# The last three stores of an attention-and-MLP kernel, issued by ScalarE instead of SyncE

## The chip, the cores and the metric

The kernel runs on one core of a Trainium2 chip. The metric is device time in microseconds of one execution. A run of the kernel is also profiled once; the profile's span goes from the first to the last instruction of the program, and the time of the execution is a little longer than that.

The engines are named as the profile names them: PE is TensorE (PEld its weight loads), DVE is VectorE, ACT is ScalarE, POOL is GpSimd, SP is SyncE. A letter q behind an engine's name marks its sequencer: the part that waits, branches, and issues DMAs. SyncE has no arithmetic; everything it does is its sequencer's.

## The reference

Two layers in a row, batch 4, 8 heads, 768 positions, 48 values a head (model width 384):

```python
# linear attention with a per-channel decay w and a bonus u for the present position
for t in range(S):
    kt, vt, rt = k[:, :, t], v[:, :, t], r[:, :, t]
    cur = np.einsum('bhd,bhe->bhde', u[None] * kt, vt)
    y[:, :, t] = np.einsum('bhd,bhde->bhe', rt, state + cur)
    state = w[None, :, :, None] * state + np.einsum('bhd,bhe->bhde', kt, vt)
...
# x is y with the heads side by side: [4, 768, 384]
xt = x.transpose(0, 2, 1)
h = xt @ U @ V                      # mixes positions, rank 32
u = x + h.transpose(0, 2, 1)
ch = np.maximum(u @ w_ch1, 0.0) @ w_ch2   # 384 -> 1536 -> 384
return u + ch
```

All inputs and the output are float32. The decays w are drawn between 0.85 and 0.95.

## The kernel before

The attention is done in chunks of 128 positions, six to a batch (`NCH`), with matmuls inside a chunk and a small state from chunk to chunk. The MLP is done in halves of a batch: a step of 384 positions (`TB`), two steps to a batch (`NTB`), three blocks of 128 rows to a step (`TPB`). For each of 12 slices of the hidden width, `m_1` multiplies (in two float parts, "high" and "low"), ScalarE takes the ReLU (line 1080), VectorE takes the remainder of it (line 1081), and `m_2` adds the second product to three accumulators in PSUM. TensorE works on the MLP of one batch while the attention of the next is slipped in between.

The order of the instructions is made by a planner written in the kernel (class `Plan`). Every piece of work is an `op` with an engine, an estimated duration and the buffers that it reads and writes; `schedule` plays them through and picks an order, and `run` then emits the instructions in that order, each engine's program being one fixed sequence. The helper `dma` (line 364) makes an op of a transfer: `eng` says whose queue issues it, SyncE's unless it says "ACT". ScalarE's queue is used so far only by a few loads at the very start. The synchronisation itself, semaphore waits of the issuing engine, is added by the framework. There are eight semaphores for the completion of DMAs, given out in turn to whatever queue issues; before a semaphore is used again, the issuing engine checks that its last transfer has landed.

The end of a step is in `m_2`. For the last step of the last batch, the matmuls are ordered block by block, so that the three accumulators end one after the other. VectorE adds each to its rows x (line 1120), and a store of 128 rows of 1536 bytes takes the result from x to the output (line 1124). The op of the store reads x, so SyncE waits for VectorE's addition before it issues.

Behind the plan there is a second way of computing everything, for decays that the fast path can't handle. `flags` (line 465, placed in the schedule at the start of the second batch) compares w with 0.7 and 1.0 and writes 1 into `flag` when any value lies outside; with the inputs here it is 0. After the plan, line 1312 has every engine load the flag from SBUF into a register (its own `TENSOR_LOAD`), and line 1313 opens `tc.If(rv == 1)` around `slow_path()`. Each engine branches for itself: with a flag of 0 it jumps over its part of `slow_path` to a short block, which the profile also puts on line 1313. There the semaphores are raised to the values that they would have after the other path. SyncE has eight such instructions, one for each DMA semaphore, each of which first checks that the transfers issued so far have landed; ScalarE, VectorE and TensorE have one each, for their own semaphore. Line 1340 is the end of the program: SyncE checks all semaphores once more, two to an instruction (the last pair has ScalarE's), and then all engines meet twice at a barrier.

`slow_path` (line 1151) itself begins with loads of w and u on SyncE's queue (lines 1163 and 1164), goes through all positions in a loop with VectorE alone, writes the attention's result to DRAM, and then runs the same MLP functions for each batch, with its stores to the output on SyncE's queue as well. None of it is executed here.

Of the kernel before, what the change touches and what calls it, by code (L numbers as in the profile page):

```python
# [46 lines left out]
class Plan:  # L47
# [28 lines left out]
    def op(self, eng, ns, fn, w=(), r=(), alt=(), lock=False, dma=0.0, rows=0, late=0.0, tiled=False, dk=0.0):  # L76


        if self.direct:
            fn()  # L80
            return None
        o = Op()
        o.n = len(self.ops)
        o.key = (self.key + dk, o.n)
        o.ways = [(eng, ns, fn, lock)] + list(alt)
        o.dma, o.rows, o.late, o.tiled = dma, rows, late, tiled
        o.deps, o.behind, o.allocs, o.bufs = set(), set(), [], []
        for acc, write in [(a, False) for a in r] + [(a, True) for a in w]:
            b, sub = acc if isinstance(acc, tuple) else (acc, None)
            if not b.uses and b.tag:  # L90
                o.allocs.append(b)
                ring = self.rings.setdefault(b.tag, {"order": [], "next": 0, "free": [(0.0, "")] * b.bufs, "last": None})
                ring["order"].append(b)
            elif b.tag and b.uses[0][0] is not o:
                o.behind.add(b.uses[0][0])
            for p, s, pw in b.uses:
                if (write or pw) and (s is None or sub is None or s == sub) and p is not o:
                    o.deps.add(p)
            b.uses.append((o, sub, write))
            if b not in o.bufs:  # L100
                o.bufs.append(b)
                b.left += 1
        self.ops.append(o)
        return o
# [184 lines left out]
def rwkv_moe(ctx: ExitStack, tc: tile.TileContext, r, k, v, w, u, U, V, w1, w2, out):  # L289
    nc = tc.nc  # L290
    B, H, S, D = r.shape
# [13 lines left out]
    NTB = S // TB  # L305
    TPB = TB // 128
# [25 lines left out]
    def bank(tag, name):  # L332
        return Buf(ps, [128, 512], F32, tag, {"mm": 2, "acc": 3}.get(tag, 1), name)
# [7 lines left out]
    def whole(*args, **kw):  # L341

        opened.clear()
        return nc.tensor.matmul(*args, **kw)  # L344
# [19 lines left out]
    def dma(fn, w_, r_, rows, run, eng="SP", ns=470, dk=0.0, late=0.0, either=False):  # L364

        q = nc.scalar if eng == "ACT" else nc.sync
        return op(eng, ns, lambda: fn(q), w_, r_, dma=rows * max(1.08 if run < 500 else 0.96, run / 400),
                  rows=rows, late=late, dk=dk, alt=[("ACT", ns, lambda: fn(nc.scalar), False)] if either else ())
# [617 lines left out]
    def inside(b, t):  # L986

        return b < B and (t == 0 or b == 0)
# [96 lines left out]
    def m_2(b, t, f, first, last):  # L1085

        hh, hl = hs.pop((b, t, f))
        for i in range(TPB):
            n = b * NCH + t * TPB + i
            if first:  # L1090
                ops[n] = bank("acc", f"p2_{n}_{f}")

        def high(i, pt):
            ts_ = slice(i * 128, (i + 1) * 128)
            for half in range(2):
                whole(pt.t[:, :DM], lhsT=hh.t[:, ts_], rhs=W2[f].t[:, half], start=(first and not gates and half == 0), stop=False)

        def low(i, pt):
            ts_ = slice(i * 128, (i + 1) * 128)
            whole(pt.t[:, :DM], lhsT=hl.t[:, ts_], rhs=W2[f].t[:, 0], start=False, stop=last > 0)  # L1100
        def gate(i, pt):
            whole(pt.t[:, :DM], lhsT=V3.t[:, (t * TPB + i) * 128:(t * TPB + i + 1) * 128], rhs=Gs[b].t, start=True, stop=False)
        gates = f == 0 and inside(b, t)
        if gates:
            for i in range(TPB):
                pt = ops[b * NCH + t * TPB + i]
                pe(MM, lambda i=i, pt=pt: gate(i, pt), [pt], [Gs[b], V3])
        parts = [(part, m, h, i) for part, m, h in ((high, 2, hh), (low, 1, hl)) for i in range(TPB)]
        if b == B - 1 and t == NTB - 1 and last:

            parts.sort(key=lambda p: p[3])
        for part, m, h, i in parts:
            n = b * NCH + t * TPB + i
            pe(m * MM, lambda part=part, i=i, pt=ops[n]: part(i, pt), [ops[n]], [h, W2[f]])
        if last:
            for i in range(TPB):
                n = b * NCH + t * TPB + i
                x, pt = xs[n], ops[n]
                s0 = (t * TPB + i) * 128
                on_dve(384, lambda e, x=x, pt=pt: e.tensor_tensor(x.t, pt.t[:, :DM], x.t, ALU.add), [x], [pt])  # L1120
                left[n] = left.get(n, NFT) - last
                if not left[n]:
                    del left[n]
                    dma(lambda q, x=x, s0=s0: q.dma_start((out[b] if b < B else slow_out[0])[s0:s0 + 128, :], x.t), [], [x],
                        128, 1536, ns=375)

    left = {}

    def mlp_units(b):

# [12 lines left out]
    slow_out = [None]  # L1143
# [7 lines left out]
    def slow_path():  # L1151
        st = xbuf([128, EQ, D], F32, "bl", 5, "s_state").t
        tmp = xbuf([128, EQ, D], F32, "bl", 5, "s_tmp").t
        wb = work.tile([128, D], F32, tag="xl", name="s_w", bufs=NXS)
        uu = work.tile([128, D], F32, tag="dv", name="s_u", bufs=2)
        rb = xpool.tile([128, TS, D], F32, tag="uTh", name="s_r", bufs=2)
        kb = xpool.tile([128, TS, D], F32, tag="uTh", name="s_k", bufs=2)
        pb = xpool.tile([128, TS, D], F32, tag="uTl", name="s_p", bufs=2)
        vb = work.tile([128, TS, EQ], F32, tag="ldv", name="s_v", bufs=3)
        yb = work.tile([128, TS, EQ], F32, tag="ldr", name="s_y", bufs=NR)  # L1160
        dg = work.tile([128, TS], F32, tag="dg", name="s_dg", bufs=2)
        for i in range(128 // H):
            nc.sync.dma_start(wb[i * H:(i + 1) * H], w)
            nc.sync.dma_start(uu[i * H:(i + 1) * H], u)
        nc.vector.memset(st, 0.0)
        rf, kf, vf = (a.rearrange("b h s d -> (b h) s d") for a in (r, k, v))

        def de(ap):
            return ap.unsqueeze(1).broadcast_to([128, EQ, D])

        def ee(ap):
            return ap.unsqueeze(2).broadcast_to([128, EQ, D])

        with tc.For_i(0, S, TS) as t0:
            for q in range(NQ):
                ps_ = slice(q * BH, (q + 1) * BH)
                nc.sync.dma_start(rb[ps_], rf[:, ds(t0, TS), :])
                nc.sync.dma_start(kb[ps_], kf[:, ds(t0, TS), :])
                nc.sync.dma_start(vb[ps_], vf[:, ds(t0, TS), q * EQ:(q + 1) * EQ])
            nc.vector.tensor_mul(pb, kb, uu.unsqueeze(1).broadcast_to([128, TS, D]))  # L1180
            nc.vector.tensor_mul(pb, pb, rb)
            nc.vector.tensor_reduce(dg, pb, AX.X, ALU.add)
            for i in range(TS):
                nc.vector.tensor_mul(tmp, st, de(rb[:, i, :]))
                nc.vector.tensor_reduce(yb[:, i, :], tmp, AX.X, ALU.add)
                nc.vector.scalar_tensor_tensor(yb[:, i, :], vb[:, i, :], dg[:, i:i + 1], yb[:, i, :],
                                               ALU.mult, ALU.add)
                nc.vector.tensor_mul(st, st, de(wb))
                nc.vector.tensor_mul(tmp, de(kb[:, i, :]), ee(vb[:, i, :]))
                nc.vector.tensor_add(st, st, tmp)  # L1190
            for q in range(NQ):
                for b in range(B):
                    p0 = q * BH + b * H
                    dst = xd[b, ds(t0, TS), :].rearrange("t (h q e) -> h t q e", h=H, q=NQ)[:, :, q, :]
                    nc.sync.dma_start(dst, yb[p0:p0 + H])
        with tc.For_i(0, B, 1) as b:
            for i in range(NCH):
                n = B * NCH + i
                x = xbuf([128, DM], F32, "x", NX, f"x_{n}")
                nc.sync.dma_start(x.t, xd[ds(b, 1), i * C:(i + 1) * C, :].rearrange("o t c -> (o t) c"))  # L1200
                xs[n] = x
            c_g(B)
            for i in range(NCH):
                c_u(B, i)
                c_ut(B, i)
            slow_out[0] = out[ds(b, 1)].rearrange("o s c -> (o s) c")
            for f in mlp_units(B):
                f()
# [61 lines left out]
    for b in range(B):  # L1270
        n0 = b * NCH
        last = b + 1 == B
        t = begin[b]
# [39 lines left out]
    with tc.If(rv == 1):  # L1313
        slow_path()
# [30 lines left out]
```

## Time and profile before

| what | us |
|---|---|
| median of three runs | 438.2 (436.89 to 439.71) |
| the profiled execution, its time | 439.95 |
| the profiled execution, its span | 437.9 |
| TensorE busy (matmuls) | 419.4 |
| VectorE busy | 267.8 |
| ScalarE busy | 142.9 |
| GpSimd busy | 55.6 |

The profile has a page, which sums up one execution, and a trace behind it, which answers questions: a timeline of a stretch, all instructions of a line, the chain of work that ended last, DMA packets by queue. A row of a line's answer reads: line, engine, operation, tiles, count, shortest/median/longest duration in ns, start of the first and of the last in us, and the shapes. A row of DMA packets reads: queue, kind, number of packets, megabytes, and their share of the 16 DMA engines' time in the stretch that was asked for; packets of the kind "instruction" carry the engines' own program code.

Two things are to be known of it here. Instructions of a sequencer (semaphore checks, branches, flag loads, issues of DMAs) are not counted as busy, and the chain of work that ended last is followed back from the last instruction that does count. And a sequencer instruction's start is when it is taken up, so a wait shows as a long instruction or as a hole in front of it.

The granted TensorE clock, in the page's row by 40 slices, is at nine tenths or more from the sixth slice (about 55 us) to the last but one, and 0.984 on average over the span.

### The profile page before, as it was taken

Reading aid. Unit: us, or ns where it says so; the run is one execution under the profiler, and the core shown is the slowest. Engines: PE = TensorE matmul, PEld = TensorE weight load, DVE = VectorE, ACT = ScalarE, POOL = GpSimd, SP = SyncE. Lnnn points to the kernel's source line nnn. Section 1 sums busy time; section 2 is a strip of 40 time slices with the busy share of each in tenths; the row PEclk is TensorE's granted clock in tenths of the full one; section 3 lists DMA queues with packets and bytes.
Section 4 is the critical chain, followed back from the end, with each engine's and each line's share of the span. In section 5 each row is a group of like instructions: output and inputs, shape, how many; then the busy total and the mean of one; then the engine's idle time right before and its main releaser. Section 6 shows DMA issues by size and latency. Waiting matters only on the chain.

```text
span 437.9 us, 12193 instructions
## 1 busy us (share of the span) xinstructions
PE 419.4 (96%) x5125; PEld 399.8 (91%) x5125; DVE 267.8 (61%) x602; ACT 142.9 (33%) x399; POOL 55.6 (13%) x92
## 2 busy tenths in 40 slices
PE   8889999999999999999999999999999999999991
PEld 8678899889999999999999999999999999999991
DVE  6979699999887757767775456567522351122121
ACT  1679679934421213121112221222112131111110
POOL 2651151223110002011100001101100000000000
PEclk9989699999999999999999999999999999999998
DMA  9979999654466876744586653231100510001001
GB/s 145 162 162 340 335 199 222 103 84 83 81 88 139 148 146 117 136 87 76 105 168 102 96 147 56 48 64 30 55 2 1 98 65 1 0 0 55 1 0 61
DMA packets 178975, 43.93 MB, mean 100 GB/s; under 512 B 168993, under 2 KB 175650, under 8 KB 178914
## 3 DMA queue, kind: packets, MB, share of 16 engines
q1 hardware_dynamic: 174162, 42.20, 46.9%
q10 hardware_dynamic: 4752, 0.89, 1.5%
q8 instruction: 42, 0.69, 0.7%
q14 instruction: 19, 0.16, 0.1%
HBM read 36.57 MB, written 6.49 MB: 98 GB/s over the span
## 4 chain that ended last, share of the span: by engine, by line
PE 81%; DVE 8%; ACT 3%; DMA 3%; POOL 1%; issue 1%; SPq 0%; ACTq 0%; DVEq 0%; POOLq 0%
PE p L344 64%; PE pav L787 5%; PE pav L793 4%; PE pu L344 3%; DVE raw_w L528 2%; DVE raw_w L525 2%; PE pab L751 2%; DMA ld<-in_r_dram 1%; DMA ld<-in_v_dram 1%; PE pab L766 1%; PE wake L344 1%; DVE hl L1081 1%; PE pG L958 1%; ACT dv L681 1%; POOL dv L671 1%
## 5 line engine op out<-in xcount | busy, mean ns | idle before, releaser
L344 PE MATMUL p<-uTh,w1s 128*128 128x384 f32 x576 | 148.2, 338 | 0.0
L1081 DVE SCALAR_TENSOR_TENSOR hl<-p,hh 128x384 fp32r<-128x384 f32 x96 | 53.2, 554 | 119.3 <-ACT hh L1080 119.0
L344 PE MATMUL p<-w2s,hh 128*128 128x384 f32 x576 | 120.3, 340 | 0.6 <-ACT hh L1080 0.6
L1080 ACT ACTIVATE hh<-p 128x384 fp32r<-128x384 f32 x96 | 47.2, 491 | 210.3 <-PE p L344 208.7
L344 PEld LDWEIGHTS p<-uTh,w1s 128*128 128x128 f32 x576 | 102.9, 188 | 0.8
L344 PEld LDWEIGHTS p<-w2s,hh 128*128 128x128 f32 x576 | 99.8, 188 | 2.8 <-ACT hh L1080 0.9
L344 PE MATMUL p<-uTl,w1s 128*128 128x384 f32 x288 | 96.4, 335 | 0.0
L344 PE MATMUL p<-w2s,hl 128*128 128x384 f32 x288 | 65.8, 335 | 0.0
L344 PEld LDWEIGHTS p<-uTl,w1s 128*128 128x128 f32 x288 | 54.0, 188 | 0.0
L344 PEld LDWEIGHTS p<-w2s,hl 128*128 128x128 f32 x288 | 51.4, 188 | 0.0
L787 PE MATMUL pav<-vsw,am 64*64 64x48 f32 x384 | 33.0, 226 | 0.6 <-DVE am L885 0.5
L793 PE MATMUL pav<-S,rT 48*64 48x48 f32 x704 | 32.0, 222 | 0.9 <-issue 0.9
L787 PEld LDWEIGHTS pav<-vsw,am 64*64 64x64 f32 x384 | 26.7, 137 | 6.1 <-issue 4.1
L751 PE MATMUL pab<-rT,kT 48*64 48x64 f32 x768 | 31.2, 228 | 0.3 <-DVE rT L721 0.2
L793 PEld LDWEIGHTS pav<-S,rT 48*64 48x64 f32 x704 | 27.9, 139 | 1.0 <-issue 1.0
L751 PEld LDWEIGHTS pab<-rT,kT 48*64 48x64 f32 x768 | 25.1, 137 | 1.5 <-DVE rT L721 0.5
L787 PE MATMUL pav<-ldv,am 64*64 64x48 f32 x320 | 26.5, 222 | 0.0
L787 PEld LDWEIGHTS pav<-ldv,am 64*64 64x64 f32 x320 | 21.5, 134 | 4.7 <-issue 3.9
L885 DVE TENSOR_TENSOR am<-pab,mask 128x256 f32<-128x256 f32 x48 | 19.7, 417 | 6.8 <-PE pav L793 6.2
L661 POOL MEMSET ks<- 128x128 f32 x24 | 4.9, 205 | 133.2 <-PE pab L766 66.8
L766 PE MATMUL pab<-ldv,ks 64*48 64x48 f32 (+1 forms) x576 | 21.0, 212 | 0.0
L926 ACT ACTIVATE SW<-S,wm 112x48 f32<-112x48 f32 x48 | 12.2, 324 | 21.3 <-DVE S L913 20.0
(127 smaller groups left out, 515.5 us busy)
## 6 DMA issues: line engine op xcount, KB each, us to landing
raw_w<-in_moe_w_ch_dram SPq DMA_DIRECT2D x24, 384.0 KB, 7.4
out_dram<-x SPq DMA_DIRECT2D x24, 192.0 KB, 2.0
ldr<-in_r_dram SPq DMA_DIRECT2D x20, 192.0 KB, 3.3
ldk<-in_k_dram SPq DMA_DIRECT2D x20, 192.0 KB, 3.6
ldv<-in_v_dram SPq DMA_DIRECT2D x20, 192.0 KB, 3.6
bl<-in_r_dram SPq DMA_DIRECT2D x79, 48.0 KB, 2.6
bl<-in_k_dram SPq DMA_DIRECT2D x79, 48.0 KB, 2.5
vsw<-in_v_dram SPq DMA_DIRECT2D x42, 48.0 KB, 3.2
```

Of the source, the lines that this page charges most:

```text
L344: return nc.tensor.matmul(*args, **kw)
L525: nc.vector.scalar_tensor_tensor(word(0), word(1), -2 ** 31, word(0), ALU.bitwise_and, ALU.bitwise_or)
L528: nc.vector.scalar_tensor_tensor(word(0), word(1), 3, word(0), ALU.logical_shift_left, ALU.bitwise_or)
L661: op("POOL", 250, lambda: nc.gpsimd.memset(ks.t[:, :, D:], 0.0), [(ks, "pad")], [])
L751: return [lambda q=q, i=i: nc.tensor.matmul(pt.t[(i ^ j) * C2:(i ^ j) * C2 + C2, q * C2:(q + 1) * C2], lhsT=kT.t[rows, q, i * C2:(i + 1) * ...
L766: return nc.tensor.matmul(pt.t[j * HP:j * HP + m, SU + q * D:SU + (q + 1) * D], lhsT=ks.t[half, 2 * q + j, :m], rhs=vt()[half, 2 * q + j, ...
L787: return nc.tensor.matmul(to(q, j, i), lhsT=am[j].t[half, q, :], rhs=vsw[n].t[half, q, :] if j else vt()[half, 2 * q, :], start=(row == RO ...
L793: return nc.tensor.matmul(to(q, row, i), lhsT=rT.t[rows, q, i * C2:(i + 1) * C2], rhs=St[n, i].t[rows, q, :], start=False, stop=(row == RO ...
L885: on_dve(256, lambda e: e.tensor_tensor(am.t, abs_[n][j].t[:, :SU].rearrange("p (h t) -> p h t", h=NP), mask_.unsqueeze(1).broadcast_to([1 ...
L926: nc.scalar.activation(dec.t[:, q], new.t[:, q], AF.Copy, scale=wm.t[:, q])
L1080: on_act(384, lambda: nc.scalar.activation(hh.t, pt.t[:, :TB], AF.Relu), [hh], [pt])
L1081: on_dve(384, lambda e: e.scalar_tensor_tensor(hl.t, pt.t[:, :TB], 0.0, f32(hh.t), ALU.max, ALU.subtract), [hl], [pt, hh])
```

## The change

The op of the store names a queue: ScalarE's for the last step of the last batch (`b == B - 1 and t == NTB - 1`, three stores), SyncE's for the 21 others. The instruction that a store emits is also kept in a list, `stored`. In `slow_path`, the first load gets a manual dependency on the last three entries of that list: until now the stores of both paths went through one queue.

```diff
-                    dma(lambda q, x=x, s0=s0: q.dma_start((out[b] if b < B else slow_out[0])[s0:s0 + 128, :], x.t), [], [x],
-                        128, 1536, ns=375)
+
+                    dma(lambda q, x=x, s0=s0: stored.append(q.dma_start((out[b] if b < B else slow_out[0])[s0:s0 + 128, :], x.t)), [], [x],
+                        128, 1536, ns=375, eng="ACT" if b == B - 1 and t == NTB - 1 else "SP")
 
     left = {}
+    stored = []
...
         for i in range(128 // H):
-            nc.sync.dma_start(wb[i * H:(i + 1) * H], w)
+            d = nc.sync.dma_start(wb[i * H:(i + 1) * H], w)
+
+            for o in stored[-TPB:] if i == 0 else ():
+                tc.add_manual_dep(d.ins, o.ins.name,
+                                  mybir.DependencyInfo(mybir.DependencyClass.Sync, mybir.DependencyReason.DATA),
+                                  reason="stored before the other path's results")
             nc.sync.dma_start(uu[i * H:(i + 1) * H], u)
```

## The prediction

> **What bounds the kernel now.** I read the page first (busy shares, then the chain that ended last), then the same chain in order of time from 341 us on, then the end engine by engine.
>
> ```profile
> span 437.9 us, 12193 instructions
> PE 81%; DVE 8%; ACT 3%; DMA 3%; POOL 1%; issue 1%; SPq 0%; ACTq 0%; DVEq 0%; POOLq 0%
> 341.42 87.62 PE p L344 x505
> 429.06 0.56 DVE x L1120
> ```
>
> TensorE carries the chain. Its last piece runs 87.62 us without a wait, and the chain ends with VectorE's third addition at 429.06 + 0.56 = 429.62 us. But the span is 437.9 us. So 8.3 us lie behind the last arithmetic, in work the page doesn't count as busy: issues of DMAs, reads of the flag, jumps, semaphore checks. The change touches this tail alone, so the tail needs its own reading. First the stores, from the timeline of the last microseconds (start, duration) and from the answers on line 1124:
>
> ```profile
> 425.93 0.49 ACT L1080 ACTIVATE hh<-p 128x384 fp32r<-128x384 f32 x1 [2.63 <-PE p L344]
> 428.01 1.60 DVE L1120 TENSOR_TENSOR x<-p,x 128x384 f32<-128x384 f32 x3 [1.00 <-PE p L344]
> 428.60 2.09 SPq L1124 DMA_DIRECT2D out_dram<-x  x3
> 430.33 0.36 SPq L1124 DMA_DIRECT2D out_dram<-x  x1
> DMA to landing us min/median/max: 2.1/2.1/2.1
> L1124 SPq DMA_DIRECT2D out_dram<-x x3: 333/344/368, 393.4 to 394.3; - x3
> ```
>
> SyncE issues the three last stores from 428.60 to 430.69 us. The fifth row belongs to the third store alone: it starts at 430.33 and has landed 2.1 us later, at 432.4. So the output is complete 5.5 us before the span ends. SyncE's job before these was the first half's stores, over at 394.3 + 0.37 = 394.7; between 394.7 and 428.6 it has nothing to do.
>
> ScalarE has nothing behind 425.93 + 0.49 = 426.4 us. Now the flag (the answer on the tile flag), which every engine reads on line 1312 before it jumps over the path not taken:
>
> ```profile
> L473 DVE CAST flag<-outside x1: 141/141/141, 106.4 to 106.4; 1x1 int32<-1x1 f32 x1
> L1312 POOLq TENSOR_LOAD <-flag x1: 498/498/498, 352.9 to 352.9; - x1
> L1312 ACTq TENSOR_LOAD <-flag x1: 476/476/476, 425.9 to 425.9; - x1
> L1312 PEldq TENSOR_LOAD <-flag x1: 487/487/487, 427.1 to 427.1; - x1
> L1312 DVEq TENSOR_LOAD <-flag x1: 795/795/795, 429.1 to 429.1; - x1
> L1312 SPq TENSOR_LOAD <-flag x1: 577/577/577, 430.7 to 430.7; - x1
> ```
>
> The flag is ready at 106.5 us, and each engine reads it as soon as its own program arrives there: GpSimd at 352.9, long before the end. SyncE arrives last, at 430.7, because its stores stand in front. Then the jump on line 1313 (the branch, and the first checks behind it), with SyncE's eight checks split by two windows, its seventh check alone, and the end on line 1340:
>
> ```profile
> L1313 ACTq COMPARE_BRANCH  x1: 50/50/50, 426.5 to 426.5; - x1
> L1313 ACTq EVENT_SEMAPHORE  x1: 17/17/17, 427.0 to 427.0; - x1
> L1313 PEldq COMPARE_BRANCH  x1: 3507/3507/3507, 427.7 to 427.7; - x1
> L1313 PEldq EVENT_SEMAPHORE  x1: 51/51/51, 431.2 to 431.2; - x1
> L1313 SPq COMPARE_BRANCH  x1: 50/50/50, 431.4 to 431.4; - x1
> L1313 SPq EVENT_SEMAPHORE  x4: 17/17/17, 434.3 to 434.5; - x4
> L1313 SPq EVENT_SEMAPHORE  x4: 17/17/17, 436.3 to 436.6; - x4
> L1313 SPq EVENT_SEMAPHORE  x1: 17/17/17, 436.5 to 436.5; - x1
> L1340 SPq EVENT_SEMAPHORE  x10: 17/28/28, 436.6 to 437.9; - x10
> ```
>
> SyncE jumps at 431.4, does its first check only at 434.3 (a hole of 2.9 us), makes four checks, and has a second hole from 434.5 to 436.3 (1.8 us). The checks are for the DMA completion semaphores; the instruction records name them, and the fifth to seventh are those of the three last stores. All three had landed by 432.4, so neither hole is a wait for a transfer. In each hole the DMA answer shows an instruction packet, in a stretch that has nothing else (432.5 to 432.7, then 434.5 to 435.0):
>
> ```profile
> q14 instruction: 1, 0.01, 9.6%
> q14 instruction: 1, 0.01, 4.9%
> ```
>
> So I read both holes as SyncE waiting for code behind its jump. What ends last is SyncE's private tail: read 430.7, jump 431.4, code, checks, end 437.9, 7.2 us in all. TensorE's own jump is over at 431.2, ScalarE's takes from 426.5 to 427.0.
>
> A page of the Trainium skill says the same of jumps (Runtime: NRT & Kernel Launch, Instruction fetch mechanics): code is fetched sequentially, and a taken branch whose target lies outside the window already fetched stalls for a DMA fetch. This trace agrees for SyncE (2.9 us) and TensorE (3.5 us), and shows a near target for ScalarE (0.5 us).
>
> **The change, part by part.**
>
> *SyncE loses three issues, and the checks of their semaphores that stand before two of them.* Its program then goes from 394.7 straight to line 1312. Flag read 0.58, branch 0.05, first hole 2.9, four checks 0.2, second hole 1.8: 5.5 us, over by about 400.2, under TensorE's 87.62 us piece. The cover is 28 us wide. Then SyncE stands at the fifth check and waits for the first of the moved stores to land. Of its 7.2 us, what stays on the path is what comes after the third store's check: 437.9 − 436.5 = 1.4 us.
>
> *ScalarE gains three issues, behind 426.4 us,* when its last activation is done. No activation queues behind them; only its flag read, jump and end do. Each issue waits for the same addition as before. Before, the three took:
>
> ```profile
> L1124 SPq DMA_DIRECT2D out_dram<-x x24: 333/371/1090, 136.0 to 430.3; - x24
> L1124 SPq DMA_DIRECT2D out_dram<-x x1: 1090/1090/1090, 429.1 to 429.1; - x1
> q8 instruction: 1, 0.02, 11.8%
> q14 instruction: 1, 0.01, 5.2%
> L651 SPq DMA_DIRECT2D bl<-in_k_dram x3: 467/468/1545, 121.0 to 122.0; - x3
> q8 instruction: 1, 0.02, 29.2%
> L618 ACTq DMA_DIRECT2D ld<-in_k_dram x3: 374/437/621, 0.8 to 5.7; - x3
> L630 ACTq DMA_DIRECT2D vsw<-in_v_dram x6: 602/638/705, 1.3 to 9.8; - x6
> ```
>
> The median store issues in 0.37 us, but the second of the last three took 1.09. The two packet rows (428.6 to 429.2) show why I don't expect that to go: two packets of code start there. The two rows below are a like case: of three loads the one at 122.0 took 1.55 against 0.47, with a code packet in 121.7 to 122.0. TensorE's jump at 427.7, which calls for its code, is not changed. So on ScalarE I take the same issue times as on SyncE: 428.60 to 430.69, third landing at 432.4. The bounds: the stall vanishes, then the third store starts at its addition's end, 429.62, and lands 2.1 later at 431.7 (0.7 earlier); or an issue on ScalarE costs what its dearest one did, 0.71 against 0.36, then 3 × 0.35 = 1.05 us later, at 433.5. I take no difference, as the nearest rows of the same engine (374 to 621 for line 618) hold SyncE's 371 at their low end and the forms that were dearer have smaller pieces.
>
> *ScalarE's tail moves behind the stores:* 430.7 + 0.58 (the dearer read) + 0.1 + 0.5 = 431.9 us, still before the landing at 432.4. TensorE is through at 431.2, VectorE stops at 429.62 plus its own read and jump:
>
> ```profile
> L1313 DVEq EVENT_SEMAPHORE  x1: 21/21/21, 430.9 to 430.9; - x1
> ```
>
> So the third landing is late next, with ScalarE half a microsecond behind it, and TensorE 1.2.
>
> *The manual dependencies* on the first load of the other path stand inside the branch not taken: no cost, unless they act outside it (a rival). *The list* of stores is Python, at build time. The planner's order up to the last additions stays, since the stores come after everything and have one queue each.
>
> **The sum.** End = 432.4 (landing) + 1.4 to 1.5 (what stands behind the check) = 433.9 against 437.9: 4.0 us less. The profiled execution took 439.95 us, 2.05 over its span; that part stays, so 436.0. The median of the three runs is 438.2 (436.89 to 439.71), the profiled one lies 1.75 above it; from the median I get 438.2 − 4.0 = **434.2 us**, 0.9% less.
>
> A rule of the Trainium skill speaks against so much (DMA: Bandwidth & Descriptors, Issuing engines are not separate DMA queues): all issuing engines feed the same 16 DMA engines, and another one saves only the sequencer's time for the issue. What that would give here is rival 4. I hold to 4.0, because what SyncE is freed for is the jump, and the two holes behind it (2.9 and 1.8 us) are longer than the issues (2.09).
>
> **The rivals.**
>
> 1. *The issue stall goes too.* Third landing 431.7 or so, end 0.7 earlier: 433.5 us. For it: the stall belongs to a moment, and ScalarE's queue might meet the code packets otherwise. Against: the same moment, the same transfers. Chance 0.17.
>
> 2. *ScalarE's jump now stalls.* Its program grows by three issues and the checks before them, so its target may fall outside the fetched code. With SyncE's hole: 431.4 + 2.9 = 434.3 us. Of SyncE's tail, the 0.9 us of line 1340 that follow its check of ScalarE would come after that (an estimate, as two thirds of the 1.3 us from 436.6 to 437.9): 435.2, a gain of 2.7, so 435.5 us. Against it: the 0.5 us jump before, over only a few dozen instructions of ScalarE. The skill's rule on branches (same page as above) is what would do this. Chance 0.09.
>
> 3. *Waiting SyncE doesn't fetch ahead,* so the second hole (1.8 us) opens after the landing. 434.2 + 1.8 = 436.0 us. Against: a code packet moves at 427.5 to 427.7, when ScalarE has jumped and stands at the end, so a waiting engine's next code seems to come. The row names no engine, though:
>
> ```profile
> q14 instruction: 1, 0.01, 15.4%
> ```
>
> Chance 0.07.
>
> 4. *Only the issues are saved:* SyncE still doesn't read before the additions, and comes at 428.6 rather than 430.7. The end moves by the 2.09 us of issues: 436.1 us. Against: the flag is ready at 106.5, and GpSimd read it at 352.9, as soon as its work was done. The rule on issuing engines (same skill, DMA page, above) would give this. Chance 0.03.
>
> 5. *The other side: the new dependency holds SyncE before its flag read,* on line 1312, rather than inside the branch. Then it can't read before the third landing: 432.4 + 7.2 = 439.6, 1.7 us later than now, 439.9 us. It decides from a wait that ends after 430.7, SyncE's present arrival. Against: the dependency is hung on an instruction behind the branch. Chance 0.04.
>
> That the stores don't move at all, I can exclude: the condition names the last batch and the last half, three blocks of 128 rows.
>
> **How the numbers follow.** My forecast's chance is 0.58, the rivals' 0.17, 0.09, 0.07, 0.03 and 0.04; 0.02 is for what I don't see. The time is the likeliest case's, 434.2. Its own range is 433.5 to 435.3, from a landing between 431.7 and 433.5. The whole range takes in rivals 1 to 4, and 0.8 us below rival 1, since the median of three runs that span 2.8 us can well lie that far off: 432.7 to 436.2. One per cent, about what a measurement of this kernel can tell from no change, is 4.4 us, so 433.8 is the bound. The forecast lies 0.4 us short of it, a third of it falls beyond by the spread of the runs (0.58 × 0.33 = 0.19), of rival 1 some 0.8 (0.14), and 0.04 of the rest: 0.37 faster. Slower by over 1% (442.6) needs more than rival 5: 0.03. Within 1%: 0.60.
>
> **What would show it.** In the profile of the changed kernel SyncE's flag read and branch should stand near 395 us, its checks 1 to 4 before 401, and checks 5 to 8 close behind the landing, near 432.5, with no hole between. The three stores should be ScalarE's, from 428.6 to about 430.7, one of them near 1.1 us. ScalarE's read should come at about 430.7, its jump take 0.5. The stretch behind VectorE's last addition should shrink from 8.3 to about 4.3 us, and everything before 428 stay as it is. I'm wrong if SyncE's read still comes behind 428 us, if ScalarE's branch takes microseconds, or if a second hole follows the landing.

## The result, and the profile after

| | median of 12 runs, us | lowest to highest | profiled execution: time, span |
|---|---|---|---|
| before | 438.94 | 436.89 to 440.63 | 439.95, 437.9 |
| changed | 435.48 | 433.17 to 436.61 | 435.4, 433.5 |

The ratio is 0.9931, with a 95% interval from 0.9911 to 0.995: 3.0 us less, between 2.2 and 3.9. The medians differ by 3.5 us. The forecast was 434.2 us (0.9% less), in a range from 432.7 to 436.2.

The changed kernel's page begins with

```profile
span 433.5 us, 12193 instructions
```

and its chain of work, in order of time, has as its last long piece (start, duration):

```profile
339.19 87.62 PE p L344 x505
```

The end of the arithmetic and the stores, from the timeline of its last microseconds (start, duration; the last row is the third store alone):

```profile
425.79 1.60 DVE L1120 TENSOR_TENSOR x<-p,x 128x384 f32<-128x384 f32 x3 [1.00 <-PE p L344]
426.38 2.21 ACTq L1125 DMA_DIRECT2D out_dram<-x  x3
428.20 0.39 ACTq L1125 DMA_DIRECT2D out_dram<-x  x1
```

And from the answers on line 1125, all three stores by duration (shortest, median, longest in ns), and the landing of the third:

```profile
L1125 ACTq DMA_DIRECT2D out_dram<-x x3: 373/389/1206, 426.4 to 428.2; - x3
...
DMA to landing us min/median/max: 3.4/3.4/3.4
```

The last addition ends at 425.79 + 1.60 = 427.39 us. I call the rest of the span the tail: 433.48 − 427.39 = 6.1 us, where it was 437.94 − 429.62 = 8.3 before (spans to a hundredth from the trace). So the tail is 2.2 us shorter, not 4.4, which is what the two spans differ by. The other 2.2 us are no part of the change: TensorE's long last piece lasts 87.62 us in both, but starts at 339.19 instead of 341.42. Two more profiles of the kernel before, below, have their additions up to 2.6 us earlier than its first one, so the way there varies. The granted TensorE clock of the first 60 us varies with it. It was 0.91 in the first profile of the kernel before and 1.00 in this one, and 1.00 in both from 60 to 425 us. Over the six profiles of the two kernels, the last addition ends between 426.9 and 427.4 us where the first 60 us were granted 0.97 or more, and between 428.6 and 429.6 us where they were granted 0.91 or 0.94. No run here sets the clock, so that it is the cause is not shown.

Next, SyncE and ScalarE. Their flag reads (the answer on the tile flag):

```profile
L1319 SPq TENSOR_LOAD <-flag x1: 558/558/558, 392.5 to 392.5; - x1
...
L1319 ACTq TENSOR_LOAD <-flag x1: 545/545/545, 428.6 to 428.6; - x1
```

Their jumps and checks, and the end of TensorE's jump (the answers on line 1320, SyncE's checks in two windows):

```profile
L1320 SPq COMPARE_BRANCH  x1: 50/50/50, 393.2 to 393.2; - x1
L1320 SPq EVENT_SEMAPHORE  x4: 17/17/17, 396.0 to 396.4; - x4
L1320 SPq EVENT_SEMAPHORE  x4: 17/17/17, 429.1 to 431.7; - x4
L1320 ACTq COMPARE_BRANCH  x1: 62/62/62, 429.2 to 429.2; - x1
L1320 ACTq EVENT_SEMAPHORE  x1: 17/17/17, 429.7 to 429.7; - x1
L1320 PEldq EVENT_SEMAPHORE  x1: 51/51/51, 429.1 to 429.1; - x1
```

And SyncE's end (line 1347, from its first and from its second check on):

```profile
L1347 SPq EVENT_SEMAPHORE  x10: 17/28/28, 431.8 to 433.4; - x10
L1347 SPq EVENT_SEMAPHORE  x9: 17/28/28, 432.2 to 433.4; - x9
```

SyncE reads and jumps at 392.5 and 393.2, right behind its last remaining store, and its 2.9 us hole (393.2 to 396.0) lies under TensorE's work. It then stands at its fifth check until 429.1, when the first moved store has landed, and passes the third store's check at 431.7. ScalarE does the three issues, reads at 428.6 and is through its jump at 429.7. The end hangs on the landing, as forecast. But the landing took 3.4 us, not 2.1, and from the check at 431.66 to the span's end it takes 1.8 us, not 1.4: there is a step of 0.4 us between the first and second check of line 1347 (431.8 and 432.2), where the others take 0.06 to 0.09.

The semaphore of the third store tells what was late. A transfer raises it by one for each of its sixteen parts (the trace has sixteen rises for each of the three stores). Fifteen came between 430.03 and 430.18, that is 1.8 to 2.0 us behind the issue. The sixteenth came at 431.65. The DMA packets that start from 429.8 to 430.6, when nearly all of the stores is out, show what shares the DMA engines with it:

```profile
q8 instruction: 1, 0.02, 8.2%
q10 hardware_dynamic: 5, 0.01, 6.0%
q14 instruction: 2, 0.02, 6.0%
```

Five packets of the stores start in that stretch (queue q10, ScalarE's), next to one packet of 16 KB and two of 8 KB of program code. The big one starts 0.7 us after TensorE has come out of its jump. The packet records tell more of the late part. Its eight rows of 1536 bytes start at 430.143 us, just as the first 8 KB packet (429.839 to 430.146) ends, and are done at 431.09. Three of them take 0.19 to 0.27 us instead of 0.07 while the two other code packets are under way (430.34 to 430.79 and 429.86 to 430.91). So the late part waits behind code packets of both sizes.

### The profile page after: what moved, and what is told of

It is laid out like the page before. It is cut to its first block, busy times and chain, and to the rows that moved or that the text cites. A ratio compares the mean times of both kernels' runs of the same rounds, so it can differ in the third digit from the quotient of the medians.

```text
span 433.5 us, 12193 instructions
## 1 busy us (share of the span) xinstructions
PE 414.6 (96%) x5125; PEld 394.8 (91%) x5125; DVE 267.7 (62%) x602; ACT 143.3 (33%) x399; POOL 56.6 (13%) x92
## 4 chain that ended last, share of the span: by engine, by line
PE 80%; DVE 12%; DMA 3%; SPq 2%; ACT 1%; POOL 1%; issue 1%; POOLq 0%
PE p L344 64%; PE pav L787 4%; PE pav L793 3%; DVE raw_w L528 3%; PE pu L344 3%; DVE raw_w L525 2%; SPq L618 2%; PE pab L751 2%; DMA ub<-in_u_dram 1%; PE pab L766 1%; DVE hl L1081 1%; DMA ldk<-in_k_dram 1%; PE pG L958 1%; DVE w2s L549 1%; DMA wT<-in_w_dram 1%; DVE uTl L1013 1%
## 5 line engine op out<-in xcount | busy, mean ns | idle before, releaser
L793 PE MATMUL pav<-S,rT 48*64 48x48 f32 x704 | 31.1, 218 | 0.9 <-issue 0.9
L793 PEld LDWEIGHTS pav<-S,rT 48*64 48x64 f32 x704 | 27.0, 135 | 1.1 <-issue 1.1
```

The costliest lines, as they stand in the source:

```text
L793: return nc.tensor.matmul(to(q, row, i), lhsT=rT.t[rows, q, i * C2:(i + 1) * C2], rhs=St[n, i].t[rows, q, :], start=False, stop=(row == RO ...
```

## The experiments

My theory: the gain is SyncE's read and jump, taken out of the tail; what is missing of the forecast is program code being fetched, which holds up one sixteenth of the stores and costs a step at a page edge. The rivals were that ScalarE's queue is the better (or the worse) one for the stores by itself, and that the steps between SyncE's checks are waits.

Each row gives, from the trace, the tail (last addition's end to the span's end), the landing of the third store counted from the last addition's end, and what lies behind the landing; times are ratios to the kernel before.

| kernel | tail, us | third landing, us | behind it, us | ratio (95% interval) |
|---|---|---|---|---|
| before, three profiles | 8.32, 8.08, 8.82 | 2.85, 2.67, 4.07 | 5.5, 5.4, 4.8 | |
| changed, three profiles | 6.09, 5.00, 5.80 | 4.26, 3.17, 3.96 | 1.84, 1.84, 1.84 | 0.9931 (0.9911 to 0.995) |
| third_on_sync | 7.83 | 1.99 | 5.8 | 1.0017 (0.9996 to 1.0037) |
| near_code | 5.23 | 3.65 | 1.58 | 0.9934 (0.9909 to 0.9959) |
| no_branch | 3.05 | 2.15 | 0.90 | 0.9889 (0.9858 to 0.992) |
| edge_moved | 6.31 | 2.88 | 3.4 | 0.9972 (0.9951 to 0.9994) |
| after_edge | 5.41 | 3.95 | 1.46 | 0.9914 (0.9882 to 0.9946) |
| code_later_8 | 4.00 | 2.54 | 1.46 | 0.9941 (0.9909 to 0.9973) |
| code_later_18 | 5.77 | 4.32 | 1.46 | 0.9925 (0.9905 to 0.9946) |

**One store left on SyncE (third_on_sync).**

```diff
-  eng="ACT" if b == B - 1 and t == NTB - 1 else "SP"
+  eng="ACT" if b == B - 1 and t == NTB - 1 and i < TPB - 1 else "SP"
```

> The changed kernel with the third of the three last stores back on SyncE's queue; the first two stay on ScalarE's. My theory: the gain comes from SyncE being free to read the flag and jump 28 us early, and one store left on it takes nearly all of that back. SyncE then issues at the third addition's end (or up to 0.7 us later, if the issue is stalled there too), and the whole tail of 7.2 us follows: stretch from the last addition's end to the span's end 7.6 to 8.3 us, a flag read of SyncE behind the additions, time 438.2 to 438.9 against 438.9 of the kernel before. Rival: ScalarE's queue is the better one for each store by itself. Then two thirds of the gain of 3.5 us stay, 436.6 us.

Its third store in the timeline:

```profile
428.42 0.33 SPq L1125 DMA_DIRECT2D out_dram<-x  x1
```

SyncE's flag read, then its jump and checks (the last row: the first seven of the eight):

```profile
L1319 SPq TENSOR_LOAD <-flag x1: 543/543/543, 428.8 to 428.8; - x1
L1320 SPq COMPARE_BRANCH  x1: 50/50/50, 429.4 to 429.4; - x1
L1320 SPq EVENT_SEMAPHORE  x8: 17/17/17, 432.6 to 434.8; - x8
L1320 SPq EVENT_SEMAPHORE  x7: 17/17/17, 432.6 to 433.1; - x7
```

With a single store left, SyncE's read, its jump (hole of 3.1 us) and its checks with a second hole (433.1 to 434.8) are back behind the additions. The tail is 7.8 us, and the time is that of the kernel before, a gain of more than 0.04% being outside the interval. Two of the three stores went through ScalarE as in the changed kernel, and brought nothing. So it isn't the queue that pays. The third store, issued by SyncE at once, landed in 2.0 us, without the second store's stall in front of it.

**The page edge in the kernel before (edge_moved).**

```diff
             nc.sync.dma_start(uu[i * H:(i + 1) * H], u)
+        for i in range(10):
+            nc.sync.dma_start(uu[i * H:(i + 1) * H], u)
```

> The kernel before, with ten more loads of u on SyncE's queue inside the path not taken (loads of the same values to the same place, never executed). They move SyncE's eight checks behind the branch by ten instructions. My theory: the second hole in SyncE's tail (1.8 us behind the fourth check) is a page edge of its code that falls four instructions behind the jump's target; moved by ten, the edge lies in front of the target, the first hole (2.9 us) stays, the eight checks follow each other in 0.1 us steps, and the tail is 6.5 us instead of 8.3: time 437.1 us against 438.9. Rival: the second hole is a wait for something that ends at that time (a transfer or another engine); then it stays where it is, tail 8.3 us, time 438.9.

SyncE's branch and its eight checks:

```profile
L1315 SPq COMPARE_BRANCH  x1: 50/50/50, 431.2 to 431.2; - x1
L1315 SPq EVENT_SEMAPHORE  x8: 17/17/17, 433.9 to 434.4; - x8
```

The first hole stays (431.2 to 433.9), the second is gone: eight checks in 0.5 us. The tail is 2.0 us shorter than in the first profile of the kernel before, and the time 0.3% less (0.06 to 0.5%). Instructions that are never executed made the kernel faster, by where they put the others. The second hole is a page edge of SyncE's code.

**The same in the changed kernel (after_edge).** The edit is the same, in the changed kernel.

> The changed kernel with the ten never executed loads of u in the path not taken, as in the run with the moved edge. In three profiles of the changed kernel 1.83 us lie between the third landing and the end, where I had put 1.45; the whole difference is one step of 0.4 us instead of 0.07 between two checks of SyncE, nine instructions behind its jump's target. My theory: that is a page edge again, with the next page already there, and it costs 0.33 us by itself. Moved by ten, it lies in front of the target; all checks behind the landing follow at 0.06 to 0.08 us, and 1.45 us lie between landing and end. Tail 4.6 to 5.7 us as the landing falls (3.2 to 4.3 us behind the last addition), time about 0.4 us under the changed kernel's, 0.992 of the kernel before. Rival: the step is a wait at that check (it names VectorE's flag read or a DMA); then it stays.

SyncE's last four checks behind the jump, and its end:

```profile
L1322 SPq EVENT_SEMAPHORE  x4: 17/17/17, 428.2 to 430.6; - x4
L1349 SPq EVENT_SEMAPHORE  x10: 17/28/28, 430.7 to 432.0; - x10
```

All steps are 0.06 to 0.07 us now, and 1.46 us lie behind the landing, where three profiles of the changed kernel have 1.84. So an edge costs 0.33 us even where the next page had more than 30 us to arrive. third_on_sync agrees on the place. Its SyncE has two instructions ahead of the branch that it doesn't have in the changed kernel (a check and an issue), and its hole lies behind the seventh check, where the step of the changed kernel lies behind the ninth. The ratio, 0.9914, is the lowest of all kernels that keep the second path; its interval overlaps the changed kernel's, so the times alone don't tell the two apart.

**The landing from run to run (after_2, after_3, before_2, before_3).** Unchanged kernels.

> The changed kernel once more, for its tail alone. My theory: the third store's landing is what the tail hangs on, and fifteen of its sixteen parts land 1.9 us behind the issue; the sixteenth depends on whether TensorE's second packet of code meets it, so the tail should be either near 4.4 to 5 us or near 6, and differ from run to run. Rival: the landing is always 3.4 us; then the tail is 6.0 to 6.2 us again.

> As the run before it: tail near 4.4 to 5 us or near 6 by my theory, 6.0 to 6.2 us by the rival.

> The kernel before once more. My theory: its tail hangs on SyncE's own read, jump and two holes, not on any landing, so it is 8.2 to 8.4 us again, whatever the third store does. Rival: it varies by a microsecond or more as the code packets fall.

> As the run before it: a tail of 8.2 to 8.4 us by my theory, a microsecond or more off by the rival.

The third store alone, in the second profile of the changed kernel:

```profile
L1125 ACTq DMA_DIRECT2D out_dram<-x x1: 390/390/390, 429.3 to 429.3; - x1
...
DMA to landing us min/median/max: 2.5/2.5/2.5
```

The landing is 2.5 us behind the issue here, 3.2 in the third profile, 3.4 in the first, and the changed kernel's tail follows it: 5.00, 5.80, 6.09. What lies behind the landing is the same to 0.01 us. The kernel before was less steady than I had said: 8.08, 8.32, 8.82. Its tail doesn't follow the landing (the third profile's came at 4.07 us, long before SyncE's checks ended), but it does go with the issue of the second store, which SyncE has to sit through: 1.00, 1.09 and 1.42 us. That is 0.42 of the 0.74 us between the shortest and the longest tail; the second hole (1.83, 1.81 and 2.01 us) has 0.18 of the rest. On average the tail went from 8.4 to 5.6 us, by 2.8. That is the gain that the times show (3.0, between 2.2 and 3.9).

The packet records say where the stall ends. In eleven profiles, the kernel before and the changed one among them, one issue starts while a 16 KB packet of code is under way, is stalled, and ends 0.37 to 0.38 us after the packet, which is about what an issue takes without a stall. It is so on SyncE's queue as on ScalarE's. The stalled one is the second issue, but in edge_moved, where the packet came 0.6 us later against the last addition, it is the third (0.79 us, with 0.58 for the second). One issue was not held up: SyncE's in third_on_sync, which starts 0.17 us before the packet's end, took 0.33 us while ScalarE's was stalled. Why, is open.

How late the third store is issued goes with how late its last sixteenth comes. Nine profiles have their next 16 KB packet 2.3 to 2.8 us behind the last addition. Where the third store was issued up to 0.71 us behind that addition, the last sixteenth came 0.02 to 0.51 us behind the others; where it was issued at 0.76 us or later, 1.08 to 1.47 us behind them. This is read from timing; no run here changes the stall alone.

**No jump at all (no_branch).**

```diff
-    rv = nc.values_load(flag.t, min_val=0, max_val=1, skip_runtime_bounds_check_because="0 or 1 by construction")
-    with tc.If(rv == 1):
-        slow_path()
```

> The changed kernel without flag read, branch and second path (lines 1319 to 1321 left out; for the decays given here the result is the same). My theory: nothing is left of the tail but the three issues of 0.35 to 0.4 us without a stall, a landing of about 2.0 us behind the last of them, one or two checks and the barriers (0.9 us): 2.9 us behind the last addition's end against 6.1, time about 432.3 us. Rival: the landing is late for a reason that has nothing to do with code being fetched (3.4 us as in the changed kernel's profile); then the tail is 5 us or more and the time about 434.5.

The three stores, and the landing of the third:

```profile
L1125 ACTq DMA_DIRECT2D out_dram<-x x3: 365/388/578, 426.4 to 427.6; - x3
...
DMA to landing us min/median/max: 2.0/2.0/2.0
```

All code packets from 426 us to the end:

```profile
q14 instruction: 1, 0.01, 0.4%
```

There is no packet on q8, the longest issue is 0.58 us instead of 1.21, and the third store lands 2.0 us behind its issue with its sixteen parts within 0.2 us. The tail is 3.05 us, and the time 1.1% under the kernel before (0.8 to 1.4%). The queue is the same, so ScalarE's queue isn't slow. One small packet is left, 0.5 us ahead of the last addition's end, as at about that time in every profile here, and it may be what makes the second issue 0.2 us longer than the others still.

**TensorE's target brought near (near_code).**

```diff
-            for f in mlp_units(B):
-                f()
```

> The changed kernel without the MLP in the path not taken (the loop over hidden slices in slow_path is left out, so that path would no longer give the result for other decays; the path that runs is whole). TensorE's program behind its branch shrinks from some 500 matmuls to some 50. My theory: the 1.2 us issue of the second store and the last sixteenth of the third store, 1.5 us late, are both TensorE's code packets, called for by its far jump. With a near target neither should be there: three issues of 0.35 to 0.4 us, third landing 1.9 to 2.1 us after its issue, TensorE's branch well under 3.5 us, tail from the last addition's end 3.4 to 3.9 us instead of 6.1, time about 432.9 us. Rival: issue and landing are slow on ScalarE's queue whatever TensorE's code does; then the tail stays at about 6 us and the time at 435.5.

TensorE's jump:

```profile
L1318 PEldq COMPARE_BRANCH  x1: 364/364/364, 426.1 to 426.1; - x1
L1318 PEldq EVENT_SEMAPHORE  x1: 51/51/51, 427.5 to 427.5; - x1
```

The stores:

```profile
L1125 ACTq DMA_DIRECT2D out_dram<-x x3: 373/390/1370, 427.0 to 429.0; - x3
```

The code packets that start between 427 and 428 us, then all that start between 428 and 433 us:

```profile
q8 instruction: 1, 0.02, 8.3%
q14 instruction: 1, 0.01, 2.6%
q14 instruction: 1, 0.01, 0.8%
```

A miss in part. From branch to first check TensorE takes 1.4 us instead of 3.7 (425.45 to 429.14 in the changed kernel), and its second packet is gone. The first is still there, at nearly the same time, with the stall (1.37 us). I take it that TensorE goes over to its next page, and that the page after that is called for, far jump or not; no run here shows it. The sixteenth part is 0.7 us late instead of 1.5, with no 16 KB packet under way. What is under way is the one 8 KB packet of the last row shown (430.05 to 430.66 us): the eight rows of the late part start at 430.659, as it ends. So a small packet delays a sixteenth, too. The tail is 5.2 us where I had 3.4 to 3.9, and the ratio (0.9934) is the changed kernel's.

**TensorE's jump moved (code_later_8, code_later_18).** The kernel after_edge, with 8 or 18 more matmuls of 128x384 behind the last one, into a bank that nothing reads:

```diff
+        if b == B - 1 and t == NTB - 1 and last:
+            spare = bank("mm", "spare")
+
+            def idle():
+                for _ in range(8):
+                    whole(spare.t[:, :DM], lhsT=hh.t[:, :128], rhs=W2[f].t[:, 0], start=True, stop=True)
+            pe(8 * MM, idle, [spare], [hh, W2[f], ops[n]], dk=1.0)
```

> The kernel with the edge moved in the changed program, and eight more matmuls of 128x384 on TensorE behind its last one (into a spare PSUM bank that nothing reads), so that TensorE reads the flag, jumps and calls for its code 8 x 0.174 = 1.4 us later. My theory: the packets of TensorE's code are what stalls the second store's issue (0.7 us) and holds up the last sixteenth of the third store. Moved by 1.4, the first packet starts at about 0.5 us behind the last addition, when the stores are issued, and the second at 3.9, when they have landed: second issue 0.6 us or less, third store issued at 0.03 to 0.2 us, its fifteen parts landed at 2.0 to 2.2, the last at 2.2 to 3.3, tail 4.0 to 4.7 us, time 433.3 to 434 against 435.5 of the changed kernel, if the kernel before is at 438.9. Rival: TensorE is still what the end hangs on, or the stall belongs to ScalarE's queue: then the 1.4 us are added or nothing changes, tail 5.2 us or more.

> The same with eighteen more matmuls, 3.1 us. My theory: no packet of TensorE's code falls among the stores, the issues take 0.37, 0.6 or less and 0.39 us, and the third store has landed at 2.1 to 2.2 us behind the last addition. But TensorE's jump now ends at 1.6 + 3.1 = 4.7 us, and SyncE's check of TensorE, with 1.0 us behind it, sets the end: tail 5.6 to 5.8 us, time as the changed kernel's within 0.3 us. Rival: the landing still comes at 3.2 us or later.

TensorE's branch with 8 matmuls:

```profile
L1329 PEldq COMPARE_BRANCH  x1: 3327/3327/3327, 424.8 to 424.8; - x1
```

and with 18:

```profile
L1329 PEldq COMPARE_BRANCH  x1: 3987/3987/3987, 426.8 to 426.8; - x1
```

With 18 also the stores, and the landing of the second:

```profile
L1132 ACTq DMA_DIRECT2D out_dram<-x x3: 373/387/777, 425.9 to 427.3; - x3
...
DMA to landing us min/median/max: 4.3/4.3/4.3
```

With 8 matmuls the edit didn't do what it was for. TensorE's sequencer runs ahead of its matmuls: the branch stands 1.87 us before the last addition's end, as against 1.94 without them, and nothing was moved. That this one profile has a tail of 4.0 us, as forecast, is luck: its landing came early (2.54 us), behind the shortest stalled issue of all kernels on ScalarE's queue (0.96 us); twelve runs, from 431.78 to 438.25, show no gain over the changed kernel.

With 18, the branch moved by 1.8 us, and the first packet of code from 0.9 us before the last addition's end to 0.9 behind it. The stall went with it: the second issue takes 0.78 us instead of 1.15. And the parts that are late changed: now the second store's sixteenth is 2.0 us behind its other fifteen (3.85 against 1.83 us) and the third's as well (4.32 against 2.34). I had expected the branch to move by 3.1 us and the stores to have landed before that packet; the packet came 1.4 us before the third store's fifteen parts had landed. The tail, 5.77 us, lies in the forecast of 5.6 to 5.8 by luck: it ends behind the late landing, as by the rival, and not behind TensorE's jump, which is over 0.4 us earlier. The late parts move when TensorE's code is moved, and are gone where nearly all code is gone (no_branch). That the 16 KB packets alone make them is not so, by near_code.

## Why the prediction was right, and by how much it was off

The mechanism was right, and two terms of the sum were too small. The median of 435.5 us lies inside the whole range (432.7 to 436.2), but just outside the range of the forecast's own case (433.5 to 435.3); what took it in were the bounds kept for the rivals, none of which happened.

- *The bound.* Right. The 8.3 us behind the last addition were SyncE's read, jump, two waits for code and checks; third_on_sync brings them back with one store.
- *SyncE's read and jump go under TensorE's work.* Right: read at 392.5, first hole from 393.2 to 396.0. That the second hole is code, edge_moved shows. That the first is code too is not shown as directly; it rests on the packets in it and on its staying where it was while the second went. Three code packets start in it (16 KB at 431.99, 8 KB at 432.10 and 432.59 us), of which the forecast showed the last; which of them is SyncE's, the trace doesn't say.
- *The three issues on ScalarE.* Right: 0.37, 1.21, 0.39 us against 0.33, 1.09, 0.36. The stall comes on either queue, and goes with the code that is fetched (no_branch, code_later_18).
- *ScalarE's own tail* ran 0.5 us ahead of the landing in the forecast. Its jump did take 0.5 us.
- *The landing.* Here the sum was mis-sized. I had taken 2.1 us from the issue, from one profile; three profiles of the changed kernel have 3.4, 2.5 and 3.2. Counted from the last addition: 3.8 us on average against 2.8. In the kernel before, a late sixteenth was without effect, since SyncE came to its checks only later, and the one execution that I read happened to have it 0.2 us late. I had priced code packets in the issue, and not in the landing.
- *Behind the check:* 1.4 to 1.5 us in the forecast from the third store's check on; 1.84 measured from the landing, nearly the same instant, for the page edge. The forecast left the second hole behind the fourth check, under TensorE's work. But with fewer instructions of SyncE ahead of the branch, the edge came behind the ninth check, and so behind the landing. after_edge, where it is out of the way, gives 1.46.
- *The sum:* of 4.0 us, 1.0 went to the landing and 0.4 to the edge; the kernel before has a tail of 8.4 rather than 8.3 on average, which gives 0.1 back. That leaves 2.7, and the times say 3.0 (2.2 to 3.9). Of the distance between forecast and median (1.3 us), 0.7 is that the kernel before measures 438.94 over twelve runs, not 438.2 over three. That the total came so near owes something to chance: the gain in the medians is 3.5 us, and in the profiles' tails 2.8.
- *The rivals.* The stall stayed (1). ScalarE's jump didn't stall (2). A waiting SyncE did fetch ahead (3): at the edge it lost 0.33, not 1.8 us. SyncE came well before the additions (4), and no wait of the new dependency stands ahead of its read (5).

The Trainium skill's rule on taken branches (Runtime: NRT & Kernel Launch, Instruction fetch mechanics) fits the traces here: behind the branch SyncE stands for 2.7 to 3.1 us and TensorE for 3.3 to 4.0 us, and TensorE, with most of the path not taken left out, for 1.4 us (near_code). How wide the fetched window is, no run here shows. Its rule on issuing engines (DMA: Bandwidth & Descriptors, Issuing engines are not separate DMA queues) holds as well, in that the queue brought nothing to the transfers. But "the time on the sequencer" that it grants was 2.1 us of issues, and what the sequencer does next was worth more: a read, a jump and the code behind it.

## What to carry to other kernels

When the span goes on for microseconds behind the last arithmetic, read the sequencers there, one by one: what each does after its last work may be a long private chain, and the engine whose queue has the last stores starts it last. Give the last stores to an engine whose own end is short, and let the one with the long end run out early, under work that covers it. And when a wait becomes the one that decides, take its length from several executions: a landing whose spread was hidden before now moves the time.

## What the runs showed of the hardware that I had not expected

- Code and data share the DMA engines, and packets of code delay one sixteenth of a store. Of the third store, that part landed up to 2.0 us behind the other fifteen with packets of 16 and of 8 KB near it (code_later_18), 0.7 us behind them with one of 8 KB (near_code), and 0.04 us behind them with none (no_branch).
- A DMA issue that starts while a 16 KB packet of code is under way can be stalled until 0.37 to 0.38 us after that packet (eleven profiles, SyncE's queue and ScalarE's; one issue in third_on_sync was not held up).
- A page edge of a sequencer's code has a price of its own: 0.33 us when the next page had 30 us to come, 1.8 us when the edge lies four instructions behind a jump. Ten instructions that never run remove it.
- TensorE's sequencer takes up its jump well ahead of its matmuls: eight more moved the branch by 0.07 us only, eighteen (3.1 us of work) by 1.8. In both runs 14 matmuls start behind the branch's own start.
